# New clocks and margins in the model of a hand-planned kernel, and an instruction order searched with them

## The chip, the cores and the metric

The kernel runs on one core of a Trainium2 chip. A core has five engines that run side by side: TensorE (PE in the profile, with its weight loads as PEld), VectorE (DVE), ScalarE (ACT), GpSimd (POOL) and SyncE (SP), which issues the DMAs here. The metric is device time in microseconds; a few runs are made and their median is given.

## The reference

Input `x` has 2048 rows of 512. Attention with 32 query heads of 16 and a single key and value head is mixed, by a gate for each row, with a gated feed-forward layer of width 1792.

```python
def _A_ref(x, wq, wk, wv, wo):
    q = (x @ wq).reshape(B, S, H, Dh).transpose(0, 2, 1, 3)
    k, v = x @ wk, x @ wv
    scores = einsum("bhqd,bkd->bhqk", q, k) * (Dh ** -0.5)
    p = softmax(scores, axis=-1)
    o = einsum("bhqk,bkd->bhqd", p, v)
    return o.transpose(0, 2, 1, 3).reshape(B, S, H * Dh) @ wo

def _B_ref(x, w_gate, w_up, w_down):
    g, u = x @ w_gate, x @ w_up
    return (sigmoid(g) * u) @ w_down

g = sigmoid((x * gate_w).sum(-1, keepdims=True))
return g * _A_ref(x, ...) + (1 - g) * _B_ref(x, ...)
```

All inputs are float32; the kernel splits operands into a high and a low part where it needs the accuracy.

## The kernel before

The queries stand in four blocks of 512 rows. A block has eight groups of four heads; a block with one group is a unit, and there are 32 units. For each unit TensorE makes the scores twice. Once with the queries on the rows of the result (`maximum`, L1108), from which VectorE takes the row maxima (L1110); the maxima of a unit are finished (L972), turned by a small transpose on TensorE (`max_turn`, L980), copied out by VectorE (L982, L983) and sent by four small DMAs (L988) into spare rows of the stacked queries `qs`. Then with the keys on the rows (`scores`, L1117), where the maxima are subtracted in the matmul itself; ScalarE takes the exponential out of the bank (L1119). The exponentials of 128 keys and four heads are multiplied with the values in one values step (`pv`, L995: four matmuls that the trace shows as eight). The sums of several values steps stay in one bank, until the sum is closed: ScalarE copies it to an `ou` tile (L1003), and GpSimd adds it to the unit's earlier part (L1006). The feed-forward layer and the output projection (`fill`, L1087) run as filler beside all this, with their own readers: `gate` (ScalarE, L1091), `gated` (VectorE, L1097) and `part_of` (ScalarE L1068, VectorE L1050). GpSimd splits weights and `h` and adds parts.

The scores, the maxima and the filler have a contraction of at most 64 rows. They run in pairs, one matmul in the upper and one in the lower half of the array; one such pair is a step. The values steps and the projections of the beginning use all 128 rows, so the array goes from one way of working to the other many times.

All results of TensorE go into eight banks (`banks`, one `[128, 512]` tile each). A bank is taken for a matmul once its last reader is done with it, and the wait for that is made by semaphores.

The order of instructions is not left to a scheduler. It is written out in the string `ORDER`, one code for each act of TensorE, found beforehand by a search. A hexadecimal digit is a step: its two base-4 digits say what each half issues (1 a maximum, 2 a score, 3 filler). `V` is a values step, `G` a projection of the beginning, `T` the turn of a unit's maxima, `C` closes a sum early, and `.` lets 25 units of the plan's clock go by without issuing anything. When the program is built, `plan` walks the string through the class `State`, a model with a clock for each engine (`now` is TensorE's). A step costs 100 units. Going from steps to full-array work costs `IN`, going back `OUT`. From these clocks the model decides which bank is taken (the one that it thinks is free first), when each helper act of the other engines and each DMA is put into their queues, and where splits, adds and stores stand. The clocks have no effect on the chip other than through this order: there every engine runs its queue in order and waits for semaphores.

The names that the change touches are the model's costs, in units:

- `RED`, `EXP`, `COPY`, `SCALED`, `GATED`: what a maximum, an exponential, a copy and the other readers keep their engine busy.
- `LATE` and `LATE_A`: from the issue of a matmul to the earliest start of its reader on VectorE and ScalarE. `close` uses `LATE` for the copy of a sum to `ou`.
- `FREE` and `FREE_A`: the margin that is put behind the end of a reader before the bank counts as free; `TAIL` and `TAIL_A` are in front of it.
- `VALUES`: what a values step costs TensorE.

The taking of a bank, for a maximum:

```python
self.free[i] = self.on("dve", self.now + LATE, RED) + TAIL + FREE
```

and in `take` the model insists on `self.free[i] <= self.now`. The difference of the two is called the plan's margin of that taking below.

Of the kernel before, what the change touches and what calls it, by code (L numbers as in the profile page):

```python
# [651 lines left out]


ORDER = (
    "GGGGGGGG555G555G555G555GGG5551GG555GG555GG555G555G555G555GT77fff7f7fffff7ffd77ffbf6fedbf7dbfbdbfdf6defedefde7b7b"
# [4 lines left out]
    "bffddd5VVVVC7b677bfefb7e7be7ffddeb7fbbe7ffed6fedfddddVVV996VV6debf7f9fb7bf9db7eff7fbdefe7efedaf7f6fdf5VVC995VVVC"
    "7ebde7fb79fbe7efdedef6b7fb7efd9fbf6edfbff55VVVa9TVVVC76feedbdfe7b7bdbfbd9fb7bf7be7fbdedeedfed7f6V965VVVV6f6fedbd"
    "fbd6fef6bf7bdede7febdbdfbdb7bfef775VVV6a9V999V65aV65aV659VVC7e6bfde7fb7bf6f9bf79fef6f6ffbTbff6ffde6eeddVa69V95aV"
    "95aV955VVVde6eedf7fbdebdbdbfdb7bb7ff6e7ef7e7bdbfff55dVVV96aV9a5VC569VVC9edff6fTffefbfbdb7f5VVC677efef9f6fffdbdbf"
    "faV699VC66ff7bf6f6fb7b7bffde7bfdbbe7ffedef5fdddddVVVVV7a7bfde7fbdedbedfb7ffbf7ef9e7f6faf7f6efddVV95aVVVC7b79fbfb"
    "dafdb7edfedbf6bf79ffe79fef9f6f6feddV9a5VV66TVVVC7b7b7bf9fbdedee7efd6fedbf6ff9f9fb7be7fef5ddVVVVV79bb7fedfb7beded"
    "fb7e7ef6fde7efbd9fedeff7776VVC699VV956VVC7b79fbbdfe7ef9dbbf7ededbbf7ededf6fe7bbffed5VV969VT65VVVC7b7e7bbdfedbb7e"
    "7bfdedeb7bfde7b7fe7ef9efdddeV6a5V65aV95aV56aV952aV999V666V966V996V966V95aV966V995VVC76bff67bfb7bfTffbdbfdedbfeed"
    "fedeedf6fb76fV695VV959VV76bb7ff9fb79fe7bffde7fe7bbdfefedeededff57VV966V996VVVC7bTbffedef9ededfe7fbdffb7bbdfeed7b"  # L670
    "e7ff7b5VVVVCdedebdb7f9fbedf6ff7fbeedff6f6f9f9fbdf7777VVV965VVC6bdff6e7fb7bdee7edfb7b7eff9b7fb7edef6fbddddVVVa95V"
    "VC7b7be7e7fedeedbbdfdbdefbd7bedfefTefbdfb7757VVVVVC7b7ee7edfbdebde7fe7b7b7efdbdbfbdb7edbfefed5VVVVVC7b7bedf9fede"
    "def6fe76fef6fb7f9bf79fbb7ffddd5VV76feb7defbdaf7f9fbd6fdVVVC7adf7ebdfbfTefbdefd776VVVVC7b7eedbdf6fbb7edefdbdfeeff"
    "7bdfbdeb77bff5dVVVVC7b7a7fedfe7edeb7fbd6fb7bff6b7fbdedede7bfdddVVVVV6bdff6b7f9f6feb7dfb6ffb7af7f9fededef9fedf79V"
    "C5a5VVVVC6b5ffeb7fedebdbdbdfbfTbfedef76eff6f9fbdf577VVVVVC7b79bfedfedbf6debf79fe7bf9fedefd6fbdeff7b5bVa96V655VVV"
    "V7b7afdedfe76ffb7bf6f9fe7bdb7e7fbdbfefeddd5eVVV6a9V9T5VVC7b7a7fedf7fbfbe7ffde7fefbf7fdeeffed9fV699V695VVVC7b7bdb"
    "e7fbdef6f6defefb7fb7fedf9fef9dbffdaV969VVVV66ff7bb7f6f6fe7efbdf7eb7ffeedbf7bdffde5ddVVVVC97feedbdfbdebd7bef7efTe"
    "fef9fdbdbf9fbdf77757VVVVVC7e7bed7efb7b7ef9bdfbdedefde7efbdb7bdbfbf6deVV659VV666VVC6dfeb7edfb7afdb7bf79fbbdff6e7d"
    "bfbdef6ffddd9VVa96V966V6a5V955VVVC7b6fb7f9fe7bedf9edfbfTefbdefde7eedeffb7b77aV669V959VV969VVVCdede6fbdf6fee7f6fe"
    "7b7ef9ef7f9efdb7be7ff797bV65aV9a5VV966V996V969V999V666V9a5V969V96aV996VCdedeedf6fedbb7fTfbffdbfbb7defb7e7ef6fb7d"  # L680
    "7VV965VVV7a77bf7efededef9bfdbfbf7f6fbdfe7edbbdf6fdV659VV965VVC66f7fe7efbd9fbbfTfff7bfbe7ef7edee7f9ffd5dVVVVC7b7b"
    "7ef6fedbbddbffdfebb7ff6f9fbd6fedffd5dVVVVVC7b7b7e7bfb7bbdbddefb7eb7e7fdefededef9bfdedeVa95VV659VVVCd6fe7ee7fedeb"
    "dbddbfb7ede7fbdeef7bdbff7b7775VVVVVCd9edfef6fe7e7ebd7bfbfTbfb7efdedef9fef977777VVVVC79eefde7f6febdbdfedbdbf9edfe"
    "7fb7bdbf6ff7775VVV6b7b7fb7fbdef9edfed7ddVVVC7adef7bdfbdebd7bfef7dTVVVC66bffdbdf6fbdebd7bfedfefbdfb7fb7ef67ffddaV"
    "VVVVC7b7b97bffedbb7e7fed9feed7fe7edbfe7bf6fafdddVVVVV7b7b7bf9fbdbf6e7fed6fef6ff9bddefe7bedfedf57VVC595VVVC7b7ee7"
    "efdebdbdef7bdbf9fb77efb79fef6bffed9deVV659VV6T9VVC6edf7ebdfbdee7f6f6fbdbdebfdbdfb7bdbedff777aV655VVVV7b7afd7ef9f"
    "6f7bfe7ef9fe7bf6b7ff9defbfeddd5eVVV6a9V9aTVC566VVC7b7bf7bdfbdefeedefdfffedb7efdfef7f7bbV956VVC796ffef9fb7eb7f9ff"
    "dddaVVC5bfb7e7bfbdeede7f6f7ddVVVV7bdef6b7fb7ef9debdf7f7bfbfedeefd9fedbfd77VVVVC66ffbdbdf6febdbdfe7bedfbd6fbdfb7e"
    "dbedff7677VVVa95VVVC6adff7f6fb7bdeedbdfefTefe7bf7edbf9dbfefb77aV95aV555VVVV76b7fbbdfe7eb7f9ef7e7ededfb7bdef9feb7"
    "ffdddaVC6a5VV956VVVC7bde7eb7fb7bf9bdedfefTbfbdfb767efef6fefede5VV95aV969V666V999VVVC79eff67bfbdeede7fede7ef9b7f7"  # L690
    "bbfd6feedff5b7bV95aV59aVV666V996V969V999V666V9a5V9a5V6a9V996VCde6edff6f9fef6fTfbffdbfb7bbdfbde7e7bfff55VVV695VVd"
    "e7e7bb7f9fbf6f9dbf7fb7fbebfdefdededeff57VV656VV6a5VC7a6ff7f6fedaf7fbTfff7bfbedefd9fedef9ff757VVVCde9eedf7fbdbbdd"
    "bf6f777VVCdbb77bfbd9fef6fededd77VVVVC7b7ba7fdfe7afddedefbdef6fbdf6fb7b7e7bfef6ddVVV99aVVVC9bdff6f9fbdbf6bdefd6fe"
    "de7fef6ef7bfTbfbfd775VVVVC766ffeb7fbdeb7dbbfde7b7eb7fe7dbfe7efbddddddVVVVVC5bfe7eedfe7ebd7b7efedebdb7ff9bf7b7b7e"
    "ffddd5VVV6b7ff9f9fedbf67efbd6feVVC7edafdbdfbdebde7fb7e77VV95TVVVC7b6dfeb7fedbf97bfe7f7bffbedf6fedef9f9ff5dVVVVC7"
    "b7ba7fdfedbb7e7e7f9fe7eff6b7f9fedededbff5dVVVVV7bdef6b7fb7bbdbdefdedbedbf77ef6fbdebdef7df9VVC666VV9T5VVC7b7bf9ed"
    "f6fee7edbfdb7bf9f7ef6f9f6fef9fbfd5dVVVVVC7a5ffbb7fedaf7bdf6f9fbf6f7be7efdedbedf9ff5eV965VVVV76efb7defbdef6b7f9f9"
    "fef9fedb7defbdee7fbf577VVV6a9V696V99TVVC7b7bededf9fffbe7bfdfffe7edefdfbfb7ff6VVC6f6f7bbdfb7bf6e7fdddeeVVVCdb9bf7"
    "bdfb7edee7fe7edbVVVV7b7b6fbdfedbdef9fedffbbdefdf9fe7ef6b7fe7bV69aV9a6Va95V6a6Va6aVV9a6VaaaVVaaTVVbaaVVabffebffaf"
    "bVVfeeffbabbbfbcVVeebbbffffffffeeffbfbfebaVVeeaaVVeaeVeeaVaaaVVaaVeeececcceccc8aaV88888VVVV"  # L700
)


# [517 lines left out]
```

## Time and profile before

| what | value |
|---|---|
| median of 3 runs | 1594.93 us (1594.89 to 1595.07) |
| the profiled execution | 1595.86 us, of which the span of the trace is 1593.1 us |
| granted TensorE clock, mean | 0.999 |
| busy: PE, DVE, ACT, POOL | 1585.1, 1393.8, 1203.4, 877.9 us |
| maxima on DVE (L1110) | 2048, 1261.3 us busy |
| exponentials on ACT (L1119) | 2048, 1043.8 us busy |
| values steps on PE (L995) | 4096 matmuls, 487.6 us busy |
| DMA | 98.10 MB, mean 62 GB/s |

The span runs from the first to the last instruction that the hardware profiler recorded; the execution's time has what lies around it too. Rows of groups give line, engine, operation and tiles, count, busy time in us, the mean of one in ns, and behind the second bar the idle time of the engine just before them with what ended it. Rows of the timeline give start and length in us; equal neighbours are merged, with their count. Rows of waits give the total in us, how many, and the longest.

### The profile page before, as it was taken

Reading aid. Unit: us, or ns where it says so; the run is one execution under the profiler, and the core shown is the slowest. Engines: PE = TensorE matmul, PEld = TensorE weight load, DVE = VectorE, ACT = ScalarE, POOL = GpSimd, SP = SyncE. Lnnn points to the kernel's source line nnn. Section 1 sums busy time; section 2 is a strip of 40 time slices with the busy share of each in tenths; the row PEclk is TensorE's granted clock in tenths of the full one; section 3 lists DMA queues with packets and bytes.
Section 4 is the critical chain, followed back from the end, with each engine's and each line's share of the span. In section 5 each row is a group of like instructions: output and inputs, shape, how many; then the busy total and the mean of one; then the engine's idle time right before and its main releaser. Section 6 shows DMA issues by size and latency. Waiting matters only on the chain.

```text
span 1593.1 us, 33707 instructions
## 1 busy us (share of the span) xinstructions
PE 1585.1 (99%) x12950; PEld 1001.1 (63%) x12950; DVE 1393.8 (87%) x2420; ACT 1203.4 (76%) x2356; POOL 877.9 (55%) x680
## 2 busy tenths in 40 slices
PE   9999999999999999999999999999999999999998
PEld 7776666556655666665754666666665466666553
DVE  6899999999899998889899989889998998988842
ACT  5277677788788777778778877778778877677797
POOL 5354554666653476567362648285764357656432
PEclk9999999999999999999999999999999999999999
DMA  7312111142111221124011212114211122111011
GB/s 239 139 51 72 39 60 32 32 121 74 38 59 30 77 72 43 34 64 133 27 55 35 72 40 70 36 45 112 84 41 53 32 76 62 51 32 44 9 37 43
DMA packets 52228, 98.10 MB, mean 62 GB/s; under 512 B 17960, under 2 KB 19240, under 8 KB 51044
## 3 DMA queue, kind: packets, MB, share of 16 engines
q1 hardware_dynamic: 52068, 95.96, 20.4%
q8 instruction: 101, 1.65, 0.5%
q14 instruction: 59, 0.48, 0.1%
HBM read 74.05 MB, written 8.90 MB: 52 GB/s over the span
## 4 chain that ended last, share of the span: by engine, by line
PE 99%; ACT 0%; DVE 0%; issue 0%; DVEq 0%; POOL 0%; ACTq 0%; POOLq 0%
PE bank L1087 31%; PE bank L995 30%; PE bank L1108 17%; PE bank L1117 16%; PE bank L849 4%; PE bank L871 0%; ACT p L1119 0%; PE bank L980 0%; PE bank L1160 0%; PE bank L919 0%; ACT x L767 0%; DVE ba L1169 0%; DVEq L1217 0%; POOL v_aug L865 0%; ACT q L941 0%
## 5 line engine op out<-in xcount | busy, mean ns | idle before, releaser
L1110 DVE TENSOR_REDUCE mx<-bank 128x1 f32<-128x512 f32 x2048 | 1261.3, 682 | 133.9 <-PE bank L1108 62.3
L1119 ACT ACTIVATE p<-bank 128x512 f32<-128x512 f32 x2048 | 1043.8, 650 | 85.7 <-PE bank L1117 46.6
L1117 PE MATMUL bank<-qs,ks 64*128 64x512 f32 x2048 | 710.6, 402 | 0.0
L1108 PE MATMUL bank<-ks,qs 62*128 62x512 f32 x2048 | 688.0, 406 | 0.0
L995 PE MATMUL bank<-p,v_aug 128*32 128x512 f32 x4096 | 487.6, 598 | 0.0
L1108 PEld LDWEIGHTS bank<-ks,qs 62*128 62x128 f32 x2048 | 341.1, 185 | 143.7 <-issue 39.2
L1117 PEld LDWEIGHTS bank<-qs,ks 64*128 64x128 f32 x2048 | 352.0, 185 | 107.1 <-DVE mx L1110 33.7
L1087 PE MATMUL bank<-wd,hl 64*128 64x512 f32 x1344 | 265.2, 393 | 0.0
L995 PEld LDWEIGHTS bank<-p,v_aug 128*32 128x32 f32 x4096 | 109.3, 109 | 244.3 <-issue 218.5
L1003 ACT COPY ou<-bank 128x512 f32<-128x512 f32 x112 | 66.2, 591 | 246.3 <-PE bank L995 185.8
L1087 PEld LDWEIGHTS bank<-wd,hl 64*128 64x128 f32 x1344 | 192.3, 185 | 18.9 <-issue 2.5
L1087 PE MATMUL bank<-xs,wu 64*128 64x512 f32 x672 | 188.7, 394 | 0.0
L1087 PE MATMUL bank<-xs,wg 64*128 64x512 f32 x672 | 183.9, 394 | 0.0
L1087 PE MATMUL bank<-x,wu 64*128 64x512 f32 x672 | 183.0, 391 | 0.0
L1087 PE MATMUL bank<-x,wg 64*128 64x512 f32 x672 | 181.6, 391 | 0.0
L1006 POOL TENSOR_TENSOR ou<-ou,ou 128x512 f32<-128x512 f32 x81 | 104.7, 1293 | 137.1 <-ACT ou L1003 136.7
L967 POOL TENSOR_TENSOR qs<-stage,qs 16x1024 fp32r<-16x1024 f32 x62 | 148.4, 2393 | 4.8
L1071 POOL TENSOR_TENSOR ba<-ba,pa_d 128x512 f32<-128x512 f32 x48 | 61.7, 1288 | 116.7 <-DVE ba L1050 77.6
L1087 PEld LDWEIGHTS bank<-x,wg 64*128 64x128 f32 x672 | 112.5, 185 | 10.5 <-issue 0.8
L1087 PEld LDWEIGHTS bank<-xs,wu 64*128 64x128 f32 x672 | 113.1, 185 | 7.9
L1087 PEld LDWEIGHTS bank<-x,wu 64*128 64x128 f32 x672 | 111.7, 185 | 9.6 <-issue 1.7
L1087 PEld LDWEIGHTS bank<-xs,wg 64*128 64x128 f32 x672 | 110.3, 185 | 7.7
(88 smaller groups left out, 1130.1 us busy)
## 6 DMA issues: line engine op xcount, KB each, us to landing
rg<-wg SPq DMA_DIRECT2D x28, 512.0 KB
ru<-wu SPq DMA_DIRECT2D x28, 512.0 KB
rd<-wd SPq DMA_DIRECT2D x28, 512.0 KB
stage<-qd SPq DMA_DIRECT2D x192, 64.0 KB
xs<-x SPq DMA_DIRECT2D x16, 512.0 KB
xf<-x_in SPq DMA_DIRECT2D x16, 256.0 KB
qd<-q SPq DMA_DIRECT2D x16, 256.0 KB
ra<-wo SPq DMA_DIRECT2D x8, 512.0 KB
```

Of the source, the lines that this page charges most:

```text
L849: nc.tensor.matmul(ps, w[:, p, part(kc)], X[b, kc][:, q, :], start=i == 0, stop=i == 3 * KC - 1)
L967: e.tensor_tensor(qs[r], stage[r], f32(qs[r]), op=ALU.subtract)
L995: nc.tensor.matmul(ps[32 * j:32 * j + 32, :], v_aug[:, c, :], PT.pop((u, c, j)), start=new, stop=last)
L1003: nc.scalar.copy(OU[i], ps)
L1006: nc.gpsimd.tensor_tensor(OU[n], OU[n], OU[i], op=ALU.add)
L1071: nc.gpsimd.tensor_tensor(BA[b, t], BA[b, t], PA.pop((b, t)), op=ALU.add)
L1087: nc.tensor.matmul(banks[i], l, r, start=at == 0, stop=at == j.n - 1)
L1108: nc.tensor.matmul(banks[i], qs_t[u % 3][r, pr, part(qt)], ks[r, kb * 512:(kb + 1) * 512], start=True, stop=True)
L1110: nc.vector.tensor_reduce(MX[u][:, pr, h, qt, kb:kb + 1], banks[i], axis=AX.X, op=ALU.max)
L1117: nc.tensor.matmul(banks[i], ks[r, part(c)], qs_t[u % 3][r, pr, :], start=True, stop=True)
L1119: nc.scalar.activation(p, banks[i], AF.Exp, scale=0.25)
```

## The change

Seven numbers of the model get other values, `close` gets its own constant for the start of the copy of a sum, and the string `ORDER` is replaced by another that was searched with the new numbers. No instruction's form changes. The line numbers of everything behind the new constant move by one.

```diff
-LATE, LATE_A, FREE, FREE_A = 190, 200, 65, 60
+LATE, LATE_A, FREE, FREE_A = 190, 200, 30, 42
...
-RED, GATED, SUM, ENDS, PARTS, INVERSE = 260, 258, 285, 60, 325, 70
-EXP, COPY, SCALED = 208, 210, 247
+RED, GATED, SUM, ENDS, PARTS, INVERSE = 258, 258, 285, 60, 325, 70
+EXP, COPY, SCALED = 206, 208, 245
...
-IN, OUT, VALUES, TURN = 52, 94, 371, 20
+IN, OUT, VALUES, TURN = 52, 94, 369, 20
...
+LATE_V = 60
...
     def close(self, u, last):
...
-        at = self.on("act", max(self.now + LATE, self.ou_free[i]), COPY) + TAIL_A
+        at = self.on("act", max(self.now + LATE_V, self.ou_free[i]), COPY) + TAIL_A
...
 ORDER = (
-    "GGGGGGGG555G555G555G555GGG5551GG555GG555GG555G555G555G555GT77fff7f7fffff7ffd77ffbf6fedbf7dbfbdbfdf6defedefde7b7b"
-    "defedbf6def9fbdfff575VVVVC7b7bb7edf6fe7bf6f6f9fee7ff9dbdbff7ffdddd5dVVVVVC99ffb7b7fe76fb7ef6f6fe7bfdeedfedbfTefe"
...
+    "GGGGGGGG555G555G555GG5551GG555GG555GG555GG555G555G555G555GT7f7f7f7ffffff7fddfffdef6bf7bbdfdff79fbf6f9f6fee77eefd"
+    "f9fb9defe7e7fbdffd5f5VVVVC9b77b6ffef6b77bfbbdf9bf7edee77b7ffdddd5VVVVC9debbddff7bde7efededefe7bd9fbdbfe777f75VVV"
...
 )
```

The codes of the two strings, counted:

| | before | after |
|---|---|---|
| steps (hexadecimal digits) | 4258 | 4259 |
| V, in how many runs | 512, 232 | 512, 201 |
| runs of one, two, three, four, five V | 91, 60, 39, 26, 16 | 59, 48, 47, 19, 28 |
| G, T | 24, 32 | 24, 32 |
| C | 81 | 92 |
| "." | 0 | 18 |

More of the change, by code (lines that the diff above doesn't have):

```diff
@@ L662 @@
[L662 to L700, printed above, removed]
+    "GGGGGGGG555G555G555GG5551GG555GG555GG555GG555G555G555G555GT7f7f7f7ffffff7fddfffdef6bf7bbdfdff79fbf6f9f6fee77eefd"
@@ new lines @@
+    "d7ef7777bVVVVVC67bfbTeff6fededbdee77bfedbdbedf9f9fbbdfbf677VV655VVVC97bfb6f7ef97be7feed7bf6f6fbb7e7efddefbdfddd5"
+    "VVVa95VVVC6b7defeb7f9bf79fe7be7e7fef9fb7e7bff9b9VC9ededdee5.VV565VVVCTeeb7f7b7be7fbde7eeddef9fef6f9fedbb77fbf7dd"
+    "5VVVa69V996VVV9b7edfb7bb7ededfbed7efe7e7edbbd7bfef76efbdd7VV956VVC9b5bfef7edbdVVC69edfef7bd77VVCTefe7b7ef9efffdb"
+    "f7f69VVC6e9f7bfdbf6edfe7ef97efffebdfde7bb7bf79ff5dVVa69V955VVV6b6ff9f7bbdedb7febdf7ffeefd9faf77ef6fb7dddVVVVVC6b"
+    "dfe7eb7dbfedbdbedbf7e7bf9ededfefTeff7b7797VVVVVC9f6edfbdef6bdef7bf9edfb7edbde7efe7fefb7bb577VV95aVVVV67b7bfbdbf6"
@@ new lines @@
+    "7e7bfbdef6fe7e7afdf97efedeb7fddddVVC699V955VVVCTbb6ff7bf9edbf7eb7e7fe7edef9fe7edefdb9ff977dVVVVVC6b7f6fedbf9f67b"
+    "f6fb7be7fedeedf97bffb6dfede7dVa69V999V999V65aV966V699VC699V696V666V699V65aV966V959VVC696fffb7bbdbdbdfebdedfffeed"
+    "fdbe7f9fe77f775VVVCTeee5cfebdbbdfdff77777aVVV6f97bfe7eedbdbfdbe7ff66.V95aVC9a5VVVC67bfe7ed9fb7bfb7fdefefee7b7dfb"
+    "dbfb7edef5dd.VVVVCTeedefdbf9f6ef7bb7b7f7ffe6ffef97bbfdbdfe5dVVVVVC9b7fb9f79fef9b7fef9f6bf7e7ef6edfe7b7fe76cddddV"
+    "VVVVC6b9fed7fedee7efdee7b7b7fb7bf6b7f9fdebff7d9dd.VVVVVC6deedef7edbf6bf7b7eb7bf7b7eeddbe7fdbdbf9fd7dVVVVVCTb7b7b"
@@ new lines @@
+    "febdedf9fbdee7ef7b7ef6dbfbdbd7efffdd55VVV67bf9fededbb7efde7ef757.VVVC9edadf7fafde7eef7b7bfbVVVC6b7bfTefedefd9fbd"
+    "bfdfbedfb7bf6f7befdedf757VVVVVC6f9fb5bf9fbededfbedf6fede7afddbf6faf7ff77757VVVVV6defedb7eedb7b7feedb7b7f9febddbf"
+    "b7fed9ef7f57VVVVVC9edfed6fee7eb7bf7b7b7fb7be7f9fbdbfTefedef5ddVVVVVC67bf6fed9fbdefb7eeddbfedb7bdbedfbddbbf7b7ed7"
+    "V656VV655VVV9e7defbdb7be7fbdafdf6fed9fbede7bdf7bf6effb75VV969VVC6Teeff7b7ffefbdef977dVVVC6bd9f7efbefff9f7ef57dVV"
+    "VC9edafdf7afd7efb7bf67efffebdf7eedb7fb7b7dddVVVVC9edf6fbde7bdbef7bf6f9bd.VV6e7fb9f7ef67bbdfede7f5d.VVVVC9adf7fed"
@@ new lines @@
+    "afde7bdfebdf6faf7edfbdb7bf9f7efb7f65.VV96aVV6aTVVVC67bbb7f7eedf6e7fef9debf76fbeddbdbf7bdbfdfdd6VVVVV6b77b7bbfbdb"
+    "dedf6feeddefbdafdf6ef7e7fb7ff5d5VVC955VVVC9fe6ffTeef9fdbdebdbdfb7bf6ef7bdafdef7efb7577VVVVVC9eddee7fbb7f6fedbb7f"
+    "9fedb7af7b7f6ffedadff6f5V99aV996V699V696V996V56aV666V9a6V696V999V996V669V6a5V6a9VVC969ffdefedebfTfefdfb9f7efe7ef"
+    "f9fe7f7b7b5b7VVVC9f97bbf7bf6e77efedef5dd.VVV9dedefb7ef9b7fe7be7ff96.V969V555VVVC9ee7b7f7bb7fb7fdedeffefbTefbfded"
+    "9bff9ff5eVVVVC6edfedbd9fee7fe7b7efdbffb7fe7edebdff797777VVVVVC67b7bfb7eedf6defedef6fe7bd9fbb7efdbdbdbf77ddVVVVV9"
@@ new lines @@
+    "e9ffdef9fbdbf6fdedf6faffde7bf7b7edff7b775VVVVC66dfedefef67efb7bb7b7fb7bdfeTfeb7fbded9fddf5VVVVVC9b9dffedef6f9fbd"
+    "bb7e7fe7e7bf6b7fb7f6ffd5ddddVVVV6ede7fe7beddef6ffb9fdfbfdefbdbdeb7ff7b7577VVVVCe7edb6ffbTefe7fb5efb7dVVC9edfedbd"
+    "ef6f6fbdb7be77b.V95aVVVVC67eeeddfeb7deb7fbe7b7b7fb7eedf9dbff6fb9fddd7VVVVV6defe6fdbf6edbf7bf9b77bfbdef9deef7ef5b"
+    "bff75dVVVVVC9edbf9dfbedf6dbfbedf6ef7ee6f7bf7bfTbf7bf75edVVVVVC6eddef9fbf9f9efd9fb7efe7b7bf6ed7bffbdb9fde77V669VV"
+    "655VVV9b7b7fbdeededf6fafdf6fede7bbdb7bfd7ef67f77ddVVVVC6b7a7ffdefffb5efbddf5VVVC9a7fedf7bfffed6fbfd7aVVCTedefb76"
@@ new lines @@
+    "fbbd7bfbf9edbffffde6ff9bdbdfbede77VVVC6e6ff7edbf9dbf6fedf7775.VVVV9f9fad7feb77bbdfedede77.VVVC67ba7ffdef9f9bdfbe"
+    "dfadf7bedfededef9f6bf77777.VV699V696V659VVVCTefe7edebdf6fbde7bdbe7fede7ebfdb7efdbfbb7775VVV996VVV9b7fe79fbf9e7fe"
+    "7af7e7efd6fedbdbbdfbb7deffdd5VVC65aVV6T9VVC97bfedb7be7e7fbdee7edbfdb7bf6e7fedbf9de7ff5dVVVVVC9edadff7edb7bfedede"
+    "bdfb7e7bb7edfe7af7f9ff775VV66aV699V65aV9a9V69aV666V966V999V9a6V669VC999VC669VVC95aff7bfef9bdfe7b7bf7efeffTefdebf"
+    "67fef75deVVVC6e77b7bf9fbdeef7e7edbdd.VV95aV9f6fbdededbb7ef7bf9f75d.VV965VVC9ded6dVVC67b7bb7f6fbfe7ffTbfbfb7eedde"
@@ new lines @@
+    "fb7fedfdd5VVVC9dededeeef7f6ffdebdb7ff9f9defbf6fbfb777777VVVVVC6dedeef7afdedef7bdbf6e7fbd9fbdbbfdf9fbfb7757VVV656"
+    "VVC9b7bedfdbf6dbedfef9edfede7ebdbd7bffe7fb77775.VVVTa6VVVC99bff6f7bbdededfbedededfe7afde77effbfb5b7777VVVVVC6b7e"
+    "fdb7bf9dbf9fbe7e7e7fede7e7b7bfe7eeddffd9VVVVVC6dbf9fe7edef6edffdbedfbdfbdbfbf9b77eff5777VVVVCTeef7b7bbddbfe7e7be"
+    "7ffdfef9fedebdfbdef7797VVVVVC66ffbde7edeedefdbf9dbfbdbdbf7adfbdfefb777577VVVV9edeedf7ef67eb7fbb7defb7bdaf7bdfb7e"
+    "f7fddfd5VVVVVCTedbfb7ededbedfebdb77efe7b7bfbde76fb7fbefd5dVVVVVC6bdfb9f7af7e7fe7af7dbefde7bf6bd7ef7bffdeddd9VVV6"
@@ L701 @@
+    "69VVV6f9f7bf9f9fedb7efbded6fedefe7bd9fbfb7edb7d77VVVC65aVVC9b7a7ffdffeedfb7bde7dVVC667feb7fedbfff9fe77ddVVVC9edf"
+    "adf7bf67bef7bfTffbfbbddef9f6fdefefd77aVV966V996VVV6a7ffdb7af7f9fedbf9bdffbefdf7eede7fb7ee7e7VV66aV9a9VaaaVVa6aVV"
+    "aa98VV9a9VaTaVeeeaeVVbfbabffebfVVefeebbeeeffbVVbbbbfffeeeefeVVbbbbbaVVaaa33fffefbfefeVaaVVaaaVVaeeecceVaeec8ccc8"
+    "888.8VVVV"
 )
```

7 lines of the change are left out of this document (4 added, 3 removed).

## The prediction

> **What bounds the kernel now.** I read the page first: its busy shares and the chain that ended last.
>
> ```profile
> span 1593.1 us, 33707 instructions
> ...
> PE 1585.1 (99%) x12950; PEld 1001.1 (63%) x12950; DVE 1393.8 (87%) x2420; ACT 1203.4 (76%) x2356; POOL 877.9 (55%) x680
> ...
> PE 99%; ACT 0%; DVE 0%; issue 0%; DVEq 0%; POOL 0%; ACTq 0%; POOLq 0%
> ```
>
> TensorE is busy for 1585.1 of 1593.1 us and the last chain runs along it from end to end. A busy PE can still be badly ordered, so next I asked the view of waits for the matmuls alone.
>
> ```profile
> PE bank L871 <- POOL v_aug L865: 1.3, 1, 1.3
> PE bank L1146 <- ACT ou_last L1144: 0.5, 1, 0.5
> PE bank L1155 <- DVE on L1153: 0.4, 1, 0.4
> ```
>
> Three waits, 2.2 us, all in the first or last few us. No matmul in the body waits for the reader of a bank. So the order decides the time, and it can become shorter in two ways only: less work on PE, or cheaper transitions between its two ways of working. The matmuls are the same in both orders (4258 and 4259 steps of two half-array matmuls, 512 values steps, 24 projections, 32 turns of maxima), so only transitions are left. The timeline of PE shows their price.
>
> ```profile
> 300.59 1.06 PE L995 MATMUL bank<-p,v_aug 128*32 128x512 f32 x8
> 301.59 0.50 PE L1117 MATMUL bank<-qs,ks 64*128 64x512 f32 x1
> 301.59 0.50 PE L1108 MATMUL bank<-ks,qs 62*128 62x512 f32 x1
> 301.93 0.39 PE L1117 MATMUL bank<-qs,ks 64*128 64x512 f32 x1
> 301.94 0.39 PE L1108 MATMUL bank<-ks,qs 62*128 62x512 f32 x1
> 302.16 0.39 PE L1117 MATMUL bank<-qs,ks 64*128 64x512 f32 x1
> 302.17 0.38 PE L1108 MATMUL bank<-ks,qs 62*128 62x512 f32 x1
> 302.49 1.07 PE L995 MATMUL bank<-p,v_aug 128*32 128x512 f32 x8
> ...
> 308.18 1.92 PE L995 MATMUL bank<-p,v_aug 128*32 128x512 f32 x16
> ...
> 310.38 0.39 PE L1117 MATMUL bank<-qs,ks 64*128 64x512 f32 x1
> ...
> 316.68 0.39 PE L1087 MATMUL bank<-xs,wg 64*128 64x512 f32 x1
> ```
>
> One values step (x8) alternates here with three half-array steps, four times between 300.59 and 308.18: 7.59 / 4 = 1.90 us a round. From 310.38 to 316.68 the order has 27 half-array steps and nothing else: 6.30 / 27 = 0.233 us a step. The chain in order of time gives a values step inside a run, by runs of four (x32) and of five (x40):
>
> ```profile
> 540.79 3.57 PE bank L995 x32
> 585.33 4.43 PE bank L995 x40
> ```
>
> The fifth costs 4.43 - 3.57 = 0.86 us. A round is then 0.86 + 3 x 0.233 = 1.56 us of work and **0.34 us for going into the full array and out again**. It also shows at the edges: 0.34 instead of 0.23 us from 301.59 to 301.93. In the plan's units (100 for a step, so 2.33 ns each) 0.34 us is 146, what IN and OUT together say.
>
> **The change part by part.** *Fewer visits.* Counted in the two order strings, runs of V fall from 232 to 201; the eleven visits of G that interrupt steps stay. 31 visits x 0.34 = **-10.5 us**, all on PE, where nothing hides it. One more step: +0.2.
>
> *VALUES 371 to 369.* This reprices the plan's clock (0.86 us / 2.33 ns = 369) and moves no instruction by itself; the 2.4 us that it takes off the plan's own end (512 x 2 units) are no gain.
>
> *Idle codes.* The new order has 18 "." of 25 units. They issue nothing; PE waits there only if the bank is really not free. Between 0 and 18 x 0.058 = 1.0 us; I take +0.5.
>
> *Eleven sums closed earlier.* C rises from 81 to 92, so ACT copies and POOL adds eleven more times. An early copy with the next taking of its bank, and the page's row of the adds:
>
> ```profile
> 111.58 0.59 ACT L1003 COPY ou<-bank 128x512 f32<-128x512 f32 x1 [3.86 <-PE bank L995]
> ```
> ```profile
> 112.70 0.40 PE L1108 MATMUL bank<-ks,qs 62*128 62x512 f32 x1
> ```
> ```profile
> L1006 POOL TENSOR_TENSOR ou<-ou,ou 128x512 f32<-128x512 f32 x81 | 104.7, 1293 | 137.1 <-ACT ou L1003 136.7
> ```
>
> That is 11 x 0.59 = 6.5 us on ACT (76% busy) and 11 x 1.29 = 14.2 us on POOL (55% busy): off the path, +0. Behind a POOL add stand splits of weights and of h, whose readiness the plan asks before it issues their matmuls. Were that cover gone, the 14.2 us would bound the cost. The DMAs are the same in number on SP's queue; only their places move.
>
> *Shorter margins.* FREE falls by 35 units (81 ns), FREE_A by 18 (42 ns), the ou copy is assumed 130 units (302 ns) earlier besides, and RED, EXP, COPY by 2 units (5 ns) for each instruction in a queue. A bank whose reader ends late now stops PE, with all that stands behind it. I followed each bank in the trace from its reader's end to the next matmul that takes it, where the old plan had little margin left: 95 reuses behind a maximum with under 10 units, 159 behind an exponential with under 20. First and last of each:
>
> ```profile
> 84.44 0.69 DVE L1110 TENSOR_REDUCE mx<-bank 128x1 f32<-128x512 f32 x1
> ```
> ```profile
> 85.37 0.40 PE L1108 MATMUL bank<-ks,qs 62*128 62x512 f32 x1
> ```
> ```profile
> 1489.43 0.68 DVE L1110 TENSOR_REDUCE mx<-bank 128x1 f32<-128x512 f32 x1
> ```
> ```profile
> 1490.32 0.39 PE L1117 MATMUL bank<-qs,ks 64*128 64x512 f32 x1
> ```
> ```profile
> 85.75 0.68 ACT L1119 ACTIVATE p<-bank 128x512 f32<-128x512 f32 x1
> ```
> ```profile
> 86.52 0.39 PE L1087 MATMUL bank<-x,wu 64*128 64x512 f32 x1
> ```
> ```profile
> 1562.34 0.93 ACT L1119 ACTIVATE p<-bank 128x512 f32<-128x512 f32 x1
> ```
> ```profile
> 1563.38 0.44 PE L1117 MATMUL bank<-qs,ks 64*128 64x512 f32 x2
> ```
>
> Behind DVE there are 0.24 and 0.21 us (the middle of the 95 is 0.20, nine in ten are over 0.14); behind ACT 0.09 and 0.11 (middle of the 159: 0.14, nine in ten over 0.107). A bank cannot pass in no time; I allow 0.05 us for it, an estimate of about half of the smallest slack shown here. Taking off 81 ns leaves 0.06 at the low tenth behind DVE; 42 ns leaves 0.065 behind ACT, less 5 ns for each exponential queued before it. The new order has 220 reuses behind a maximum and 265 behind an exponential with under 40 units (164 and 322 before). So perhaps one in ten to one in four of 485 stops PE by 10 to 50 ns: 0.5 to 6 us, and since a stop gives every later bank the same time more, the lower part is the likelier. I take **+2.0**. The ou banks are safe: the pair above shows 112.70 - 112.17 = 0.53 us of slack with 77 units of plan margin, and 0.38 less leaves 0.15. Eleven of 123 have under 80 units in the new plan: a few tenths of a us at most.
>
> *Turns of the maxima.* Here the old plan was too early, not too late:
>
> ```profile
> 775.21 0.43 PE L1087 MATMUL bank<-x,wg 64*128 64x512 f32 x2
> 775.74 0.22 PE L980 MATMUL bank<-consts,mm 64*16 64x64 f32 x2
> ```
>
> 0.53 us from the step to the turn instead of 0.23: PE stood 0.30 us for the finished maximum. Eight of the 32 turns had under 80 units of margin in the old plan; two have in the new one. Six times 0.1 to 0.3 us: **-1.0** (between -1.8 and 0).
>
> **The sum**, against the profiled execution (1595.86 us with a span of 1593.1): -10.5 + 0.2 + 0.5 + 2.0 - 1.0 = -8.8, so 1587.1. The median of the runs shown, 1594.93, lies 0.9 under that execution, so I forecast **1586.1 us**. With every unknown at its low end (-10.5 + 0.2 - 1.8 + 0.5 = -11.6) it is 1583.3; with 4 us at the banks and no gain at the turns 1589.1. Two runs of this kernel can be told apart from about 0.2%, 3.2 us.
>
> **The rivals.** *ACT falls behind its new clock.* EXP is now 206 units, 479 ns. Exponentials stand in rows; after ten of them the plan is 47 ns earlier than the old one, besides the 42. Of 0.09 to 0.11 us nothing is then left. If half of the 265 reuses lose 45 ns, that is 6.0 us instead of 2.0: 1590.1. For it: both ACT pairs above are under the middle. Against: a stop lets ACT catch up. Chance 0.11.
>
> *DVE becomes the bound; no change.* The saved time might come back as waiting for maxima:
>
> ```profile
> L1110 DVE TENSOR_REDUCE mx<-bank 128x1 f32<-128x512 f32 x2048 | 1261.3, 682 | 133.9 <-PE bank L1108 62.3 <-PE bank L1087 45.7 <-PE bank L1117 22.1
> ```
>
> DVE is 87% busy, and if its rows of maxima had no gap the order could not be compressed: 1594.9. Against it, DVE stood 133.9 us before its maxima, for PE; 10.5 can be taken from that. Chance 0.06. The Trainium skill speaks for this rival (TensorEngine Tiling (Array Packing), section Performance Considerations): tiling speeds up TensorE but not the emptying of PSUM, which may become the bottleneck. By that rule alone the gain would be nothing; the idle time in the row speaks against it so far.
>
> *Every short reuse stops PE; slower.* If the bank's real return is longer than I read, the 485 reuses all lose 30 ns: 14.6 us instead of 2.0, so 1598.7. Its price turns the gain into a loss from (8.8 + 2.0) / 485 = 22 ns a reuse. Against it are the slacks of 0.14 and more in nine of ten at DVE. Chance 0.05.
>
> *Late maxima.* Three units now begin their scores 10 units after the plan has the maxima landed (one before). SP issues these:
>
> ```profile
> L988 SPq DMA_DIRECT2D qs<-mt x128: 623/635/1894, 77.1 to 1543.5; - x128
> ```
>
> An issue that takes 1.89 instead of 0.64 us stops PE for 1.26; three times: +3.8, 1589.9. Chance 0.04. That the order does not do what it says is no case here: the new order has the 31 visits fewer in its instruction lists.
>
> **How the numbers follow.** The forecast has 0.74 (1583.3 to 1589.1), the rivals 0.11, 0.06, 0.05 and 0.04. The range of 1583.3 to 1591.0 takes in the first, the ACT clock and the late maxima, and leaves out no change and slower, 0.11 in all, and some tails. Faster by over 0.2% (under 1591.7): 0.74 + 0.11 + 0.04, less a tail of 0.02, 0.87. Within 0.2%: 0.06 and 0.02 of tail, 0.08. Slower: 0.05.
>
> **What would show it.** Right: the span is 8 to 10 us shorter; L995 appears in 201 runs; a round as above still costs 0.34 us; the matmuls' own waits for DVE and ACT stay under 4 us; DVE's idle time before L1110 shrinks by about the gain; L1003 stands at x123 and L1006 at x92. Wrong: PE's steps after a short reuse come at 0.26 us and more in their hundreds, first behind L1119 (ACT's clock) or L1110 (DVE); or L1117 stands at a unit's first scores; or the visits cost less than 0.34 us where the runs are longer.

## The result, and the profile after: slower by 0.65%

The new kernel takes 1605.66 us (median; 1604.67 to 1605.99) and the old one 1595.15 (1594.89 to 1595.26). The ratio is 1.0065, with a 95% interval of 1.0052 to 1.0078. The forecast was 1586.1. One correction to the description of the change: lines between the new constant and the string move by one, those behind the string by two (L1087, L1108, L1110, L1117, L1119 become L1089, L1110, L1112, L1119, L1121).

The page of the new kernel, first its span, its busy shares, the granted clock and the chain that ended last:

```profile
span 1604.2 us, 33684 instructions
...
PE 1595.9 (99%) x12950; PEld 1015.7 (63%) x12950; DVE 1395.4 (87%) x2420; ACT 1195.5 (75%) x2367; POOL 891.8 (56%) x691
...
PEclk9999999999999999999999999999999999999999
...
PE 99%; DVE 0%; DMA 0%; ACT 0%; SPq 0%; issue 0%; DVEq 0%; ACTq 0%
```

Nothing here tells that something is wrong: the same 12950 matmuls and weight loads, a TensorE that is busy for 99%, a chain that runs along it. It is busy for 10.8 us longer, and the span is 11.1 us longer. The view of waits for the matmuls says even less:

```profile
PE bank L873 <- POOL v_aug L867: 1.3, 1, 1.3
PE bank L1148 <- ACT ou_last L1146: 0.5, 1, 0.5
PE bank L851 <- ACT wq L897: 0.5, 1, 0.5
PE bank L1157 <- DVE on L1155: 0.4, 1, 0.4
PE bank L1110 <- ACT q L943: 0.2, 1, 0.2
```

Five waits, 2.9 us, none for the reader of a bank in the body. The Trainium skill (Perfetto Trace Analysis, section "Tensor Engine Instruction (MATMUL, LD_WEIGHTS)") says why a stop can be missing here: a TensorE record begins where the matmul begins to read, its wait in the queue lies before that, and its end is an estimate. This trace agrees: TensorE is busier by 10.8 us with the same matmuls.

The costliest groups:

```profile
L1112 DVE TENSOR_REDUCE mx<-bank 128x1 f32<-128x512 f32 x2048 | 1261.8, 681 | 138.3 <-PE bank L1110 67.4
L1121 ACT ACTIVATE p<-bank 128x512 f32<-128x512 f32 x2048 | 1035.6, 672 | 52.3 <-PE bank L1119 31.7
L1008 POOL TENSOR_TENSOR ou<-ou,ou 128x512 f32<-128x512 f32 x92 | 119.0, 1294 | 136.4 <-ACT ou L1005 136.0
L1005 ACT COPY ou<-bank 128x512 f32<-128x512 f32 x123 | 72.3, 588 | 296.7 <-PE bank L997 223.0
```

VectorE's idle time before the maxima did not shrink (133.9 to 138.3). On ScalarE the idle time before the exponentials went from 85.7 to 52.3 us and their mean from 650 to 672 ns: they stand closer together now. The wait rows of the weight loads moved too. First the kernel before, then the new one:

```profile
PEld bank L1117 <- ACT p L1119: 24.3, 47, 0.8
PEld bank L1108 <- ACT p L1119: 23.7, 40, 0.8
PEld bank L995 <- DVE mx L1110: 3.5, 10, 0.4
```
```profile
PEld bank L1119 <- ACT p L1121: 29.3, 104, 0.8
PEld bank L1110 <- ACT p L1121: 23.6, 88, 0.8
PEld bank L997 <- DVE mx L1112: 18.7, 58, 0.4
```

The totals hide it (48.0 us before, 52.9 now); the counts show it: 87 loads of scores and maxima were last released by an exponential before, 192 are now.

What one of them costs is seen in the timeline. On ScalarE, a copy of a sum and the exponential behind it; then TensorE in the same stretch:

```profile
364.97 0.59 ACT L1005 COPY ou<-bank 128x512 f32<-128x512 f32 x1 [0.71 <-PE bank L997]
365.45 0.61 ACT L1121 ACTIVATE p<-bank 128x512 f32<-128x512 f32 x1
```
```profile
365.58 0.40 PE L1089 MATMUL bank<-wd,hl 64*128 64x512 f32 x2
365.82 0.39 PE L1110 MATMUL bank<-ks,qs 62*128 62x512 f32 x1
...
366.11 0.49 PE L1119 MATMUL bank<-qs,ks 64*128 64x512 f32 x1
...
366.69 0.39 PE L1110 MATMUL bank<-ks,qs 62*128 62x512 f32 x1
366.92 0.39 PE L1119 MATMUL bank<-qs,ks 64*128 64x512 f32 x1
```

The exponential ends at 365.45 + 0.61 = 366.06, and the step at 366.11 takes its bank, 0.05 us later. That step starts 0.29 us behind the one before it, 0.06 late. Then two steps follow in 0.58 us (366.11 to 366.69) where 0.46 is due: **the next step is late by another 0.11**, though its own banks were long free. From there a step takes 0.23 again. A stop that reads as 0.06 us costs 0.17.

So I gave every pair of neighbouring acts of TensorE (a step, a V, a turn) the distance that undisturbed rows show (0.232 us from step to step, 0.858 from V to V, 0.34 more for a run of V) and set each distance in the trace against it. What is above is lost. A *short reuse* is the taking of a bank that its reader left less than 0.165 us ago; a loss is put down to it when it happened at that step or one step earlier:

| | work at undisturbed distances | lost at short reuses | other losses | span |
|---|---|---|---|---|
| before | 1567.3 | 3.1 (155 reuses) | 6.9 | 1593.1 |
| after | 1555.6 | 24.8 (652 reuses) | 8.0 | 1604.2 |

(Some 16 us at both ends make up the rest.) The work became 11.7 us shorter, a little more than forecast. The short reuses took 21.7 back. By reader, 20.0 us of the new kernel's loss stand behind exponentials (511 reuses), 3.6 behind maxima (101), 1.6 behind copies to `ou` (15); a step touched by two reuses counts with both here.

The price follows the *slack*, the time from the reader's end to the taking matmul's start. Single short reuses, with none beside them; the mean delay of the following step:

| slack, ns | after: count, delay in ns | old order, other banks (below) |
|---|---|---|
| 52 to 56 | 98, 74 | 98, 76 |
| 60 to 80 | 28, 49 | 33, 40 |
| 80 to 100 | 39, 42 | 55, 44 |
| 100 to 120 | 58, 33 | 61, 32 |
| 120 to 140 | 167, 21 | 107, 21 |
| 140 to 160 | 104, 11 | 93, 10 |
| 160 to 180 | 66, 2 | 56, 4 |
| 180 to 240 | 249, 1 to 2 | 266, 0 to 2 |

Slack is never under 52 ns: there the taking matmul waits itself, and in the clear cases the next step is late by 104 to 107 ns. Up to 160 ns the taking matmul is on time and only the step behind it is late.

### The profile page after: what moved, and what is told of

The parts are those of the page before. It is cut to its first block, busy times and chain, and to the rows that moved or that the text cites. A ratio compares the mean times of both kernels' runs of the same rounds, so it can differ in the third digit from the quotient of the medians.

```text
span 1604.2 us, 33684 instructions
## 1 busy us (share of the span) xinstructions
PE 1595.9 (99%) x12950; PEld 1015.7 (63%) x12950; DVE 1395.4 (87%) x2420; ACT 1195.5 (75%) x2367; POOL 891.8 (56%) x691
## 4 chain that ended last, share of the span: by engine, by line
PE 99%; DVE 0%; DMA 0%; ACT 0%; SPq 0%; issue 0%; DVEq 0%; ACTq 0%
PE bank L1089 32%; PE bank L997 29%; PE bank L1119 17%; PE bank L1110 17%; PE bank L851 3%; DMA wqr<-wq 0%; DVE mx L1112 0%; PE bank L982 0%; PE bank L1162 0%; SPq L754 0%; PE bank L921 0%; ACT x L769 0%; DVE ba L1171 0%; DVE h L1099 0%; DVEq L1219 0%
## 5 line engine op out<-in xcount | busy, mean ns | idle before, releaser
L1112 DVE TENSOR_REDUCE mx<-bank 128x1 f32<-128x512 f32 x2048 | 1261.8, 681 | 138.3 <-PE bank L1110 67.4
L1121 ACT ACTIVATE p<-bank 128x512 f32<-128x512 f32 x2048 | 1035.6, 672 | 52.3 <-PE bank L1119 31.7
L1119 PE MATMUL bank<-qs,ks 64*128 64x512 f32 x2048 | 721.6, 410 | 0.0
L1110 PE MATMUL bank<-ks,qs 62*128 62x512 f32 x2048 | 696.1, 410 | 0.3 <-ACT q L943 0.2
L997 PE MATMUL bank<-p,v_aug 128*32 128x512 f32 x4096 | 481.3, 597 | 0.0
L1119 PEld LDWEIGHTS bank<-qs,ks 64*128 64x128 f32 x2048 | 347.9, 184 | 133.3 <-issue 33.0
L1110 PEld LDWEIGHTS bank<-ks,qs 62*128 62x128 f32 x2048 | 344.9, 184 | 126.9 <-issue 32.7
L1005 ACT COPY ou<-bank 128x512 f32<-128x512 f32 x123 | 72.3, 588 | 296.7 <-PE bank L997 223.0
L1089 PE MATMUL bank<-wd,hl 64*128 64x512 f32 x1344 | 273.5, 393 | 0.0
L1089 PEld LDWEIGHTS bank<-wd,hl 64*128 64x128 f32 x1344 | 195.7, 185 | 13.2 <-issue 0.8
L1008 POOL TENSOR_TENSOR ou<-ou,ou 128x512 f32<-128x512 f32 x92 | 119.0, 1294 | 136.4 <-ACT ou L1005 136.0
L1089 PE MATMUL bank<-x,wu 64*128 64x512 f32 x672 | 190.5, 394 | 0.0
L1089 PE MATMUL bank<-xs,wu 64*128 64x512 f32 x672 | 188.9, 393 | 0.0
L1089 PE MATMUL bank<-xs,wg 64*128 64x512 f32 x672 | 184.7, 393 | 0.0
L1089 PE MATMUL bank<-x,wg 64*128 64x512 f32 x672 | 181.7, 393 | 0.0
L1089 PEld LDWEIGHTS bank<-x,wu 64*128 64x128 f32 x672 | 112.8, 185 | 5.6 <-ACT ou L1005 0.2
L1089 PEld LDWEIGHTS bank<-xs,wu 64*128 64x128 f32 x672 | 112.0, 185 | 5.0 <-POOL wd L744 0.2
L1089 PEld LDWEIGHTS bank<-xs,wg 64*128 64x128 f32 x672 | 110.2, 185 | 4.5
L1089 PEld LDWEIGHTS bank<-x,wg 64*128 64x128 f32 x672 | 108.5, 185 | 5.9 <-ACT p L1121 0.6
```

The source lines that it names most:

```text
L997: nc.tensor.matmul(ps[32 * j:32 * j + 32, :], v_aug[:, c, :], PT.pop((u, c, j)), start=new, stop=last)
L1005: nc.scalar.copy(OU[i], ps)
L1008: nc.gpsimd.tensor_tensor(OU[n], OU[n], OU[i], op=ALU.add)
L1089: nc.tensor.matmul(banks[i], l, r, start=at == 0, stop=at == j.n - 1)
L1110: nc.tensor.matmul(banks[i], qs_t[u % 3][r, pr, part(qt)], ks[r, kb * 512:(kb + 1) * 512], start=True, stop=True)
L1112: nc.vector.tensor_reduce(MX[u][:, pr, h, qt, kb:kb + 1], banks[i], axis=AX.X, op=ALU.max)
```

## The experiments

**Theory:** the order's gain is real, and is eaten because the plan now takes banks less than 0.16 us after their readers. Most of that stands behind the copies to `ou`: `LATE_V` starts them too early in the model, and all exponentials queued behind a copy are then early with it. **Rivals:** the constants themselves do harm whatever the order; the loss comes from the new order's other features and short reuses are only a sign of it; VectorE sets the pace; the margins and the exponential's clock do it without the copies.

### The constants with the old order

```diff
 # after.py, with the string ORDER of before
-        assert self.free[i] <= self.now
+        assert self.free[i] <= self.now + 20
```

> The old order with the new constants: the clocks, margins and LATE_V of the change stay, the string ORDER is that of before (two takings that the new model finds 18 units short are let through). Theory A (the loss comes from the order: many more banks are taken less than about 160 ns after their reader's end, and then the weight load of the next pair comes late): the old order has 155 such takings, so 1595 us, within 2. Rival B (the constants themselves do it, by another choice of banks or other places of helper acts): near the 1605 us of the changed kernel.

Measured: 1595.24 us (1594.81 to 1596.01), ratio 1.0 (0.9991 to 1.0009). 3.3 us are lost at 148 short reuses. The constants alone do nothing; the cause lies in the order that was searched with them.

### Shorter exponentials, in the new and in the old order

```diff
-        nc.scalar.activation(p, banks[i], AF.Exp, scale=0.25)
+        nc.scalar.activation(p[:, :256], banks[i][:, :256], AF.Exp, scale=0.25)
 # pv: reads the 256 columns twice, so that its matmuls keep their size
-            nc.tensor.matmul(ps[32 * j:32 * j + 32, :], v_aug[:, c, :], PT.pop((u, c, j)),
+            nc.tensor.matmul(ps[32 * j:32 * j + 32, :].rearrange("p (a n) -> p a n", a=2), v_aug[:, c, :],
+                             PT.pop((u, c, j))[:, :256].unsqueeze(1).to_broadcast([P, 2, 256]),
```

Both kernels leave out half of each exponential, so only their time is of use, not their result.

> The changed kernel; each exponential is taken of 256 of its 512 columns, and the values step reads these twice, so that TensorE's instructions stay the same in number, order and size while ScalarE's readers let go of their banks earlier. Theory A: the losses behind ScalarE's readers that I count in the trace of after (20.0 us behind exponentials, 2.2 behind its other readers) go, those behind VectorE (3.9) stay: 1605.5 - 22 = 1583.5 us, within 2. Rival C (the new order is slower by something that no reader makes, for instance dearer steps or visits): at most the 3.5 us go by which steps themselves start late, so 1602 us or more.

> The kernel of before with the same shortened exponentials (256 of 512 columns, read twice). Theory A: it loses only 2.7 us behind exponentials, so 1595 - 2.7 = 1592.3 us, within 1; the two orders then stand as forecast, the new one 9 us faster. Rival C: the new order stays slower by some 10 us also with short exponentials. A third case, that a shorter exponential speeds the kernel up in another way, would show as the same drop in both.

Measured: 1591.25 us (1590.59 to 1592.44) in the new order, ratio to the kernel before 0.9974 (0.9964 to 0.9985); 1592.91 (1592.39 to 1594.62) in the old one, 0.9986 (0.9977 to 0.9996). The old order behaved as expected. The new one fell by 14.4 us, not by the 22 expected. The groups of the new order with short exponentials:

```profile
span 1588.9 us, 33710 instructions
...
L1113 DVE TENSOR_REDUCE mx<-bank 128x1 f32<-128x512 f32 x2048 | 1255.6, 683 | 133.4 <-PE bank L1111 70.2
L1122 ACT ACTIVATE p<-bank 128x256 f32<-128x256 f32 x2048 | 721.4, 385 | 274.9 <-PE bank L1120 148.1
```

The loss behind exponentials is gone (20.0 to 0.3 us, in 4 reuses). That behind maxima rose from 3.6 to 8.5 (101 to 189 reuses). A likely reading, not tested by itself, is that TensorE's stops for ScalarE had been giving VectorE time, and that with them gone the cut of `FREE` shows too. 10.3 us are left lost.

### Shorter maxima as well

This kernel leaves out a quarter of each maximum too.

```diff
-        nc.vector.tensor_reduce(MX[u][:, pr, h, qt, kb:kb + 1], banks[i], axis=AX.X, op=ALU.max)
+        nc.vector.tensor_reduce(MX[u][:, pr, h, qt, kb:kb + 1], banks[i][:, :384], axis=AX.X, op=ALU.max)
```

> As the changed kernel with shortened exponentials, and each maximum is taken of 384 of its 512 columns as well. Theory A: the 3.9 us behind VectorE's readers go too: 1579.6 us, within 2. Rival D (short exponentials only move the waits to VectorE, which becomes the bound): without this the run above stays over 1590, and this one drops by 5 us or more against it.

Measured: 1581.86 us (1580.97 to 1582.02), ratio 0.9914 (0.9899 to 0.9929); 2.3 us over the 1579.6 expected, just outside its 2 us.

```profile
span 1580.2 us, 33557 instructions
...
L1113 DVE TENSOR_REDUCE mx<-bank 128x1 f32<-128x384 f32 x2048 | 1033.2, 552 | 318.2 <-PE bank L1111 156.0
L1122 ACT ACTIVATE p<-bank 128x256 f32<-128x256 f32 x2048 | 719.7, 385 | 269.3 <-PE bank L1120 133.3
```

2.4 us are still lost, about half of it behind the copies. With the readers out of the way the new order is 11.05 us faster than the old order with short exponentials (1592.91, where 1.1 us were lost). The old order was not run with short maxima as well; its 1.1 us are what short reuses could still give back there, so the gain from fewer visits comes out at 10 to 11 us, near the forecast's. The work at undisturbed distances is 1555.4, as in the changed kernel, and the other losses are some 6 us, no more than the 6.9 of the kernel before: nothing else in the new order holds time back.

### The same old order, only with other banks

```diff
-        i = self.free.index(min(self.free))
-        assert self.free[i] <= self.now
+        there = [i for i in range(8) if self.free[i] <= self.now]
+        i = max(there, key=lambda i: self.free[i]) if there else self.free.index(min(self.free))
+        assert self.free[i] <= self.now + 20
```

The new constants and the string of before, as in the first experiment, but a matmul takes the bank that came free last, not first.

> The old order with the new constants, as in the run that came out at 1595.2 us, with one edit in take: of the banks that the model finds free it takes the one that came free last, not first. TensorE's instructions are the same in number, order and size, and the other engines' queues stand in the same order; only the bank each matmul writes differs. Theory A (a bank that is taken under about 160 ns after its reader's end costs 160 ns less the slack, on the next pair): the new model lets 270 takings through with under 10 units of margin and 219 with 10 to 20, and with the slacks of the trace (about 95 ns at no margin behind VectorE and ScalarE, none behind the copy of a sum) their losses add up to 37 us if each stood alone; since a stop gives the banks behind it the same time more, I expect half of that: 1595 + 19 = 1614 us, between 1607 and 1628. Rival C (the order is what costs, not the slack of the banks): 1595 us, within 2.

Measured: 1617.40 us (1616.79 to 1617.77), ratio 1.0135 (1.0118 to 1.0152), within what was expected.

```profile
span 1615.8 us, 33693 instructions
...
PE 1605.7 (99%) x12950; PEld 988.1 (61%) x12950; DVE 1407.1 (87%) x2420; ACT 1212.0 (75%) x2356; POOL 878.5 (54%) x680
```

All engines' queues are those of the first experiment, which took 1595.24; only the bank of each matmul differs, and with it the slack behind the readers. That costs 22.2 us. 24.3 us are lost at 712 short reuses: exponentials 308 (10.3), maxima 258 (6.7), copies 88 (8.6). The price by slack is that of the changed kernel (the table above). So the short reuse is the cause and not a sign of something else in the new order. Which engine reads the bank does not matter: single reuses with 80 to 140 ns of slack, and nothing but steps around them, delay the following step by 30 ns in the mean behind ScalarE (88 of them) and by 34 ns behind VectorE (77).

### Margins mended, the order searched again

Three kernels keep the idea of fewer visits and take other numbers; each starts from the new order and is searched again with its own. All also set `ENDS` to 110 and delay a turn until 100 units after its maxima, and in their model a bank, or a V's exponentials, that is not ready yet delays TensorE's clock, where the model of the change forbids the act.

```diff
 # all three mended
-LATE, LATE_A, FREE, FREE_A = 190, 200, 30, 42
+LATE, LATE_A, FREE, FREE_A = 190, 200, 60, 69
-RED, ... EXP, COPY, SCALED = 258, ... 206, 208, 245
+RED, ... EXP, COPY, SCALED = 260, ... 208, 210, 247
-LATE_V = 60
+LATE_V = 122
```

> The changed kernel's order, mended by exchanges of neighbouring codes under other margins: FREE 60, FREE_A 69, LATE_V 122 and the old RED, EXP, COPY, SCALED, so that the model's free time stands about 160 ns behind a reader's real end, and a taking before that delays the model's TensorE instead of being forbidden. ENDS is 110, and a turn of maxima waits for 100 units more. The order has 202 runs of V (201 in the changed kernel, 232 before), 88 C and no idle codes. Theory A: TensorE's work and visits stay those of the changed kernel (10.2 us under before), and the losses at banks fall from 26.8 us to about 9 (before 3.5), with 1 to 2 us less at the turns: 1591.5 us, 0.2% under before, within 2. Rival (the slack that is needed is not 160 ns, or takings interact otherwise): the losses stay over 15 us and the run is slower than before, over 1597.

```diff
 # the start of the copy alone
-LATE_V = 60
+LATE_V = 155
```

> An order searched anew, from the new one, with one of the change's numbers put right and the others kept: LATE_V 155 in place of 60, by the measured start of the copy to ou (0.295 us after the last values step), which puts the copy and all that is queued behind it on ACT 95 units (0.22 us) later in the model. FREE 30, FREE_A 42, RED 258, EXP 206 stay. 201 runs of V, 92 early sums. What it has of V work is that of the new order. Theory (a bank taken less than 0.16 us after its reader costs 0.16 us less its slack; most of the loss is behind the copies, since the model starts them too early, and the rest from FREE_A, FREE and EXP): the 20 us lost behind exponentials falls to 7 to 12, all losses to 10 to 16, so 1597 (1593 to 1600). Rival, that the margins and the exponential's clock make the loss by themselves and the start of the copy is nothing: 1603 to 1606. Rival, that the start of the copy is all of it: losses as of the old order, 1584 to 1587.

```diff
 # the margins and the exponential's clock alone (LATE_V stays 60)
-LATE, LATE_A, FREE, FREE_A = 190, 200, 30, 42
+LATE, LATE_A, FREE, FREE_A = 190, 200, 60, 75
-RED, ... EXP, COPY, SCALED = 258, ... 206, 208, 245
+RED, ... EXP, COPY, SCALED = 260, ... 210, 210, 247
```

> The other half: an order searched anew, from the new one, with LATE_V 60 kept as in the change, but FREE 60, FREE_A 75, RED 260, EXP 210, COPY 210, SCALED 247, so that the margins and the exponential's clock are about those of before or wider. 201 runs of V, 92 early sums. Theory: behind a copy the plan is still about 0.16 us early, and 75 units less that leave a part of the exponentials under 0.16 us; no drift adds to it: 8 to 14 us are lost in all, 1594 (1591 to 1598). Rival, that the start of the copy makes nearly all of the loss whatever the margins: 1600 to 1606. Rival, that margins and the exponential's clock were all of it: losses under 5 us, 1584 to 1588.

| | time | ratio | work | lost at short reuses | slack of exponentials at the zero of the plan's margin, by their place behind a copy on ScalarE: 1-3, 4-8, 9-16, over 16 |
|---|---|---|---|---|---|
| before | 1595.15 | | 1567.3 | 3.1 | 184, 171, 148, 97 ns |
| after | 1605.66 | 1.0065 (1.0052 to 1.0078) | 1555.6 | 24.8 | 53, 34, 55, 57 |
| all three mended | 1595.36 | 1.0004 (0.9995 to 1.0013) | 1555.5 | 13.7 | 154, 145, 106, 89 |
| copy's start alone | 1602.53 | 1.0047 (1.0031 to 1.0064) | 1555.2 | 15.1 | 144, 148, 37, 22 |
| margins and clock alone | 1594.63 | 0.9998 (0.9988 to 1.0007) | 1556.1 | 14.6 | 115, 119, 138, 139 |

The last column is the slack that the chip gives where the plan thinks that it has none to spare (the median of reuses with up to 60 units of margin, less the margin). Right behind a copy the changed kernel is at the floor of 52 ns, 131 ns under before; the later start of the copy gives most of it back (144, 148), the wider margins alone give half (115, 119). Far behind a copy the slack runs out with the late copy alone (37, then 22) and does not with the wider margins (138, 139). Two things blur this. `LATE_V` of 155 is 28 units over the measured start of the copy (0.295 us, which is 127 units), so that run has 65 ns to spare there. And the third kernel changed `FREE_A` together with `EXP`: the 33 units more of `FREE_A` are 77 of its 101 to 117 ns, so the two are not told apart.

In microseconds: of the loss behind exponentials, the kernel with the copy's start mended has 1.3 at the first eight and 10.8 further on; the one with the margins mended 8.3 and 4.3. The changed kernel has 9.6 and 9.9. So both errors are at work, the copy's start near the copies and the margins with the clock behind them, in roughly equal parts, and neither rival that makes one of them everything holds. How a step touched by two reuses is counted moves these shares; the numbers of short reuses in the rows behind copies say the same: 215 at the first eight and 286 further on in the changed kernel, 17 and 165 with the copy's start mended, 145 and 106 with the margins. The totals do not show the halves: mending both left 13.7 us lost, hardly less than mending one (15.1 and 14.6).

The kernel with all three mended missed its expectation: 1595.36 where 1591.5 within 2 was expected, with 13.7 us lost where about 9 were. It did not reach its rival's numbers either (over 15 us lost, over 1597).

The kernel with the copy's start mended missed its expectation by 5.5 us, too. Its loss at short reuses (15.1) lies within what was expected, and the trace shows most of the miss elsewhere. The matmuls' waits and two rows of its timeline:

```profile
PE bank L1092 <- POOL wd L747: 1.5, 1, 1.5
PE bank L1092 <- POOL wd L748: 1.3, 2, 0.7
```
```profile
743.89 0.73 PE L1092 MATMUL bank<-wd,hl 64*128 64x512 f32 x3 [1.50 <-POOL wd L747]
744.23 0.40 PE L1122 MATMUL bank<-qs,ks 64*128 64x512 f32 x1
```

At one place filler matmuls came before GpSimd had split their weights. Four late steps there lose 3.7 us. The second row shows the aftermath of a stop once more, where no bank is involved: 744.23 - 743.89 = 0.34 us to the next step in place of 0.23.

All three have the whole gain of the work, and none is faster than the kernel before: what they lost at short reuses, 13.7 to 15.1 us, cancels it. The likely reason is that the search takes each reuse to the edge that its model allows, so that an optimistic number is met everywhere and not now and then; no run tests this by itself. An order that keeps both the 201 runs and the slack of 0.16 us was not found; whether one exists stays open.

## Why the prediction was wrong

- **Fewer visits, -10.5: right.** The work at undisturbed distances fell by 11.7 us. Of that, 31 x 0.34 = 10.5 are the visits; the rest probably goes with the places of the turns, which the forecast did not count (14 stand at an edge of a run of V now, 9 before), and some half of it comes back behind them (below). With short readers the order is 10 to 11 us faster. A round still costs what it did; the first and the last values step of four rounds in the new kernel are 7.57 / 4 = 1.89 us apart:

```profile
482.40 0.64 PE L997 MATMUL bank<-p,v_aug 128*32 128x512 f32 x4
...
489.97 0.64 PE L997 MATMUL bank<-p,v_aug 128*32 128x512 f32 x4
```

- **Early sums at no cost: right as to GpSimd, but ScalarE was not off the path.** L1005 and L1008 stand at x123 and x92, as forecast, and GpSimd held nothing up in the changed kernel. "Off the path" fails on ScalarE: 496 of the 511 short reuses behind exponentials (19.2 of 20.0 us) stand in a row of ScalarE that begins with a copy and has no gap since. Before, it was 34 (0.7 us). To stand in such a row is not yet to be short because of the copy: by the runs above that holds for about half. What the eleven copies more cost by themselves was not measured.
- **Turns, -1.0: right at the turn, hardly in the sum.** Waits at the turns fell from 1.8 to 0.7 us. But the second step behind a turn is 0.08 us late in both kernels, and 31 turns have steps behind them now, 24 before (the others went straight into V): some 0.6 us more lost there.
- **Bank stops, +2.0: the step that failed. It measured +21.7.** Two errors are in it. The first: "a bank cannot pass in no time; I allow 0.05 us". A reuse that short is not free, it is one that stops: 52 ns is the floor. The price begins at 0.16 us and falls on the next step, so it cannot be seen on the taking matmul, where I looked. By that, the middle of the slack behind exponentials was already at the edge before the change. The 0.14 and the 0.09 were read a little low besides: they go to the start of the step, and the matmul that takes the bank can be the later one of its two. In the first of the two pairs the filler at 86.52 goes on with a sum in its own bank; the score beside it takes the exponential's, 0.13 us after 86.43:

```profile
86.56 0.42 PE L1117 MATMUL bank<-qs,ks 64*128 64x512 f32 x1
```

Read so, the middle of the 159 is 0.16, and nine in ten are over some 0.12. The second error: the 130 units of the copy's earlier start were checked against the `ou` banks only ("safe"; they cost 1.6 us). In the plan they move every exponential that is queued behind a copy as well. In both traces the copy starts 0.295 us after the last values step should be done: before, the model had it 63 units too late, and that was a hidden margin of the exponentials; with `LATE_V` it is 67 units too early. The prediction let one in ten to one in four of 485 reuses stop PE; 652 were short.
- **ACT falls behind its new clock (0.11): half of the truth.** Exponentials in a row follow at 482 ns in the mean and the model's 206 units are 479, and the slack falls with the place behind a copy. But 3 ns a place are some 50 ns over 16 places, and the fall is over 100 with 206 units (144 to 37) and 87 before, with 208 (184 to 97); what takes the rest is open. And its 6.0 us was a third of what exponentials cost: its 45 ns a reuse are near the measured 39 (20.0 us / 511), but it let half of 265 lose them, where 511 were short, and it left out the copies.
- **DVE becomes the bound (0.06): no**, though its condition is near: with ScalarE relieved, the maxima took 8.5 us. The rule of the Trainium skill beside this rival (TensorEngine Tiling (Array Packing), section Performance Considerations), that the emptying of PSUM may become the bottleneck, is borne out in part: the emptying of the banks did take the gain, but both readers stand idle before their work (138.3 and 52.3 us), and it is the instant at which a bank is released that binds, not the readers' rate.
- **Every short reuse stops PE; slower (0.05): this is what happened**, with a price of 24.8 us / 652 = 38 ns a reuse, over the 22 ns from which it decided. "The slacks of 0.14 and more" that I set against it begin under the 0.16, and the change took 0.08 from them.
- **Late maxima (0.04): no.** No score waited for its unit's maxima.
- **What would show it.** The sign named for a wrong forecast, steps at 0.26 us and more behind L1121 in their hundreds, is there: 279 steps, 183 of them behind an exponential, against 33 before. One sign named for a right one, own waits of matmuls under 4 us, was there too: it does not tell the two apart.

The clock can be left out. The Trainium skill (TensorE: Matmul & The Clock Gate, section "A second HAM failure mode: psum-queue depth-cycling") tells of a kernel where short idles at PSUM made the clock go up and down. Here 652 short reuses left it at 1.0 over the whole span.

## What to carry to other kernels

Measure the price of a buffer's reuse on the instruction behind the one that takes it, and read it from the distance between starts, not from the view of waits: here a stop that read as 0.06 us cost 0.17, and matmuls showed 2.9 us of waits where 24.8 us were lost. Before a margin in a planner is cut, look for the errors that it has been paying for (here a copy that the model started 63 units too late), and follow each clock to all that is queued behind it. An order that is searched with an optimistic model can pay an error of 0.1 us hundreds of times: here short reuses went from 155 to 652.
